# Pooled attention and top-2 adapters on one core: attention closer behind the scores, the up-projection one slot later, small routing groups at both ends, later keys by bf16 transposes, first blocks interleaved

## The chip, the core and the metric

One core of a Trainium2 chip runs the whole program. The metric is device time in microseconds (us) of one execution; each kernel was executed several times, and one execution was recorded by the hardware profiler. The span of the profile (first to last instruction) is 1.7 to 2.4 us shorter than the time of the same execution. On one core a run is called slow when it is over 1.5% above the fastest of the same kernel. PE is the matmul engine (TensorE), DVE VectorE, ACT ScalarE, POOL GpSimd, and SP the queue that issues most DMAs.

## The reference

```python
kv_pool = kv.reshape(B, H//4, 4, W//4, 4, C).mean(axis=(2, 4))   # B=4, 384x32 positions, C=128
k = v = kv_pool.reshape(B, -1, C) @ w_sr                          # 768 keys per batch
a = softmax(q @ k.T / sqrt(C));  x = a @ v                        # 12288 queries per batch
logits = x @ w_gate                                               # 8 experts, the top 2 kept
out = x + sum over the two kept experts of w_e * (x @ A[e]) @ B[e]   # rank 16
```

The kernel handles 512 queries at a time: 96 chunks, numbered 0 to 95, 24 of them per batch.

## The kernel before

The main loop is a sequence of slots. In slot k the scores of chunk k are made, while earlier chunks pass through the later stages. An engine takes its instructions in the order in which they are written down. Cut:

```python
def attend(k, s):        # 6 matmuls for one quarter of the chunk, into the only accumulator buffer
def normalize(k):        # VectorE: reciprocal, multiply -> xn
def top(k):              # VectorE: 4 MAX8, the sorted logits
def route(k0, step):     # a group of (mostly) 4 chunks
    if step == 0:        # GpSimd: two subtractions, one add; ScalarE: tanh; GpSimd: a comparison
    else:                # GpSimd: two multiply/add steps -> gw, the gates
def transposes(kx, kh, tail):  # PE: xn of chunk kx and the gated hg of chunk kh; copied by
                               # VectorE, or by ScalarE in the tail (after the last scores)
def down(k), gate(k)     # PE: x @ A for all experts; VectorE: times the gates -> hg
def up(k), finish(k)     # PE: hg @ B; VectorE: plus xn; store
# ... cut ...
for k in range(LA, last + 2):                 # LA = 4
    ka, kn = k - LA, k - LA - 1               # attention 4 slots behind the scores
    scores(k, 0); normalize(kn); transposes(x_, h_, not ks)
    scores(k, 1); attend(ka, 0); top(kn); route(first[kn], 0)   # route: if a group ends here
    scores(k, 2); up(h_); finish(h_); route(first[kn], 1)
    down(x_); gate(x_); attend(ka, 1..3)
    # ... pooling adds of the next batch on GpSimd, 2 or 3 a slot, in slots 9 to 20 of a batch
    # ... pieces of key preparation at the end of slots 18 to 23 of a batch, one or two a slot
```

(The guards for the first and last slots are left out of this outline.)

The softmax here doesn't subtract the row's maximum and nothing guards it: scores larger than these inputs give would overflow.

## Time and profile before

| | before |
|---|---|
| time, median of the first three runs | 434.14 us |
| span of the profile | 431.2 us |
| PE busy | 401.7 us, 93% |
| VectorE, ScalarE, GpSimd busy | 73%, 68%, 38% |

Two parts of the page of the kernel before: the slices (each digit is the busy share of one of 40 equal slices of the span, in tenths; PEclk is the granted matmul clock in tenths), and the chain of waits that ended last.

```profile
PE   4778999999999999999999999999999999999763
...
PEclk9899999999999999999999999999999999999996
...
PE 78%; DVE 8%; ACT 6%; issue 2%; POOL 2%; SPq 2%; DMA 1%; POOLq 0%; ACTq 0%; DVEq 0%
```

PE is full from about the fourth slice to the 37th. What can be gained lies in the length of a slot, in the first four slices and in the last three.

One plain slot of PE in the timeline of the kernel before. The columns are start, busy time, instructions; the difference of two starts is what a step costs, because matmuls overlap and their ends are modelled.

```profile
59.67 0.59 PE L67 MATMUL sg<-qT,kfT 128*128 128x512 bf16 x2
60.10 0.39 PE L67 MATMUL tt_ps<-id_bf,xn 128*128 128x128 bf16 x4
60.33 0.39 PE L67 MATMUL tt_ps<-id_bf,hg 128*128 128x128 bf16 x4
60.55 0.59 PE L67 MATMUL sg<-qT,kfT 128*128 128x512 bf16 x2
60.98 0.54 PE L67 MATMUL acc<-vx,em 128*128 128x137 f16 x6
61.44 0.59 PE L67 MATMUL sg<-qT,kfT 128*128 128x512 bf16 x2
61.87 0.39 PE L67 MATMUL d_ps<-b_bf,tts 128*128 128x128 bf16 x4
62.09 0.39 PE L67 MATMUL h_ps<-a_bf,tts 128*128 128x128 bf16 x4
62.31 1.28 PE L67 MATMUL acc<-vx,em 128*128 128x137 f16 x18
```

The next slot begins at 63.43, so the slot is 3.76 us. The first six attention matmuls (60.98 to 61.44) take 0.46 us, while eighteen of them take 1.12, that is 0.37 for six: 0.09 are lost, and in the list of waits the weight loads (PEld) wait for the normalised tile (xn) 66 times, for 22.2 us in all.

VectorE's list of waits in the kernel before (total us, times, longest us):

```profile
DVE osb L340 <- PE d_ps L67: 56.0, 94, 1.9
...
DVE hg L327 <- POOL gw L292: 2.2, 3, 1.2
```

VectorE waits for the up-projection (d_ps) in nearly every chunk, and hardly ever for gates (gw).

### The profile page before, as it was taken

To read this page: it belongs to the slowest core of one execution; us is meant where nothing else is said; L and a number is where in the kernel's file an instruction comes from. 1 tells how busy PE (TensorE), PEld (TensorE's weight loads), DVE (VectorE), ACT (ScalarE), POOL (GpSimd) and SP (SyncE) were. 2 spreads that over 40 slices of the span, in tenths; PEclk is the share of its full clock that TensorE was granted. 3 is DMA by queue.
4 is the path that set the end of the run, shared out by engine and by line. 5 is a ranking of instruction groups with operands and counts; after the bars stand their busy time and mean duration, and the time that the engine had idled before them with its cause. 6 is when DMAs were issued, how large, how long until landed. Compare 5 with 4: busy or idle time off the path is not lost.

```text
span 431.2 us, 11431 instructions
## 1 busy us (share of the span) xinstructions
PE 401.7 (93%) x4589; PEld 311.3 (72%) x4589; DVE 315.4 (73%) x916; ACT 293.8 (68%) x335; POOL 165.0 (38%) x263
## 2 busy tenths in 40 slices
PE   4778999999999999999999999999999999999763
PEld 4446677777777787777777787777777778777652
DVE  2442478878777887877878888877878788888863
ACT  3349977857687777757687777767678777777422
POOL 0020278764112369764112369764202202212131
PEclk9899999999999999999999999999999999999996
DMA  8998978997459999997559998977548724422332
GB/s 267 378 244 181 248 183 154 267 176 148 124 122 213 215 270 220 242 213 148 133 114 228 242 299 227 216 162 148 143 104 172 173 74 123 111 63 75 99 98 75
DMA packets 127429, 76.44 MB, mean 177 GB/s; under 512 B 50480, under 2 KB 126512, under 8 KB 127024
## 3 DMA queue, kind: packets, MB, share of 16 engines
q1 hardware_dynamic: 126384, 64.11, 57.6%
q0 software_dynamic: 704, 11.54, 15.7%
q8 instruction: 36, 0.59, 0.6%
q14 instruction: 17, 0.14, 0.1%
q10 hardware_dynamic: 288, 0.07, 0.1%
HBM read 50.53 MB, written 36.70 MB: 202 GB/s over the span
## 4 chain that ended last, share of the span: by engine, by line
PE 78%; DVE 8%; ACT 6%; issue 2%; POOL 2%; SPq 2%; DMA 1%; POOLq 0%; ACTq 0%; DVEq 0%
PE acc L67 31%; PE sg L67 26%; PE tt_ps L67 8%; PE h_ps L67 5%; PE d_ps L67 5%; ACT em L233 4%; DVE xn L250 3%; PE kfT_ps L67 2%; PE kpT_ps L67 1%; SPq L93 1%; DMA kvr<-in_kv_dram 1%; PE v_ps L67 1%; DVE vx L213 1%; ACT tts L311 1%; DVE kpT L197 1%
## 5 line engine op out<-in xcount | busy, mean ns | idle before, releaser
L233 ACT ACTIVATE em<-sg 128x1024 f16<-128x1024 f32 x288 | 274.6, 1023 | 86.3 <-PE sg L67 86.3
L67 PE MATMUL acc<-vx,em 128*128 128x137 f16 x2304 | 174.5, 224 | 3.4 <-DVE xn L250 2.1
L67 PE MATMUL sg<-qT,kfT 128*128 128x512 bf16 x576 | 171.1, 380 | 4.7 <-ACT em L233 2.6
L67 PEld LDWEIGHTS <-em 128*128 128x128 f16 x2304 | 151.7, 98 | 30.8 <-DVE xn L250 19.7
L340 DVE TENSOR_TENSOR osb<-d_ps,xn 128x512 f32<-128x512 f32 x96 | 66.4, 691 | 56.0 <-PE d_ps L67 56.0
L167 POOL TENSOR_TENSOR kvr<-kvr 128x512 f32<-128x512 f32 x63 | 78.2, 1273 | 0.0
L250 DVE TENSOR_TENSOR xn<-acc,rinv 128x544 f32<-128x544 f32 x96 | 69.6, 725 | 3.3
L67 PEld LDWEIGHTS <-tts 128*128 128x128 bf16 x768 | 50.7, 98 | 24.6 <-ACT tts L311 2.1
L327 DVE TENSOR_TENSOR hg<-h_ps,gw 128x512 bf16<-128x512 f32 x96 | 65.4, 681 | 4.0 <-POOL gw L292 2.2
L67 PEld LDWEIGHTS <-kfT 128*128 128x128 bf16 x576 | 49.7, 97 | 17.6 <-issue 6.3
L313 DVE COPY tts<-tt_ps 128x1024 bf16<-128x1024 bf16 (+1 forms) x89 | 60.6, 683 | 0.0
L67 PEld LDWEIGHTS <-xn 128*128 128x128 bf16 x384 | 29.2, 98 | 25.3 <-DVE xn L250 2.5
L67 PE MATMUL tt_ps<-id_bf,xn 128*128 128x128 bf16 x384 | 37.1, 219 | 3.8 <-DVE xn L250 2.2
L67 PE MATMUL d_ps<-b_bf,tts 128*128 128x128 bf16 x384 | 37.4, 220 | 2.0 <-ACT tts L311 1.7
L67 PE MATMUL tt_ps<-id_bf,hg 128*128 128x128 bf16 x384 | 37.2, 220 | 1.5 <-DVE hg L327 1.5
L67 PE MATMUL h_ps<-a_bf,tts 128*128 128x128 bf16 x384 | 37.1, 219 | 0.6 <-ACT tts L311 0.4
L269 DVE MAX8 srt<-xn 128x8 f32<-128x8 f32 x384 | 34.9, 153 | 0.3
L245 DVE RECIPROCAL rinv<-acc 128x4 f32<-128x4 f32 x96 | 17.3, 180 | 17.8 <-PE acc L67 14.3
L67 PEld LDWEIGHTS <-hg 128*128 128x128 bf16 x384 | 25.4, 98 | 2.1 <-DVE hg L327 2.1
L311 ACT COPY tts<-tt_ps 128x1024 bf16<-128x1024 bf16 (+1 forms) x10 | 8.0, 844 | 15.4 <-PE tt_ps L67 12.8
L171 DVE TENSOR_TENSOR kvr<-kvr 128x512 f32<-128x512 f32 x12 | 7.7, 687 | 6.3 <-DMA kvr<-in_kv_dram 6.2
L213 DVE CAST vx<-v_ps 128x272 f16<-128x272 f32 x12 | 5.3, 445 | 9.1 <-PE v_ps L67 9.0
(244 smaller groups left out, 175.0 us busy)
## 6 DMA issues: line engine op xcount, KB each, us to landing
kvr<-in_kv_dram SPq DMA_DIRECT2D x96, 256.0 KB, 5.0
out_dram<-osb SPq DMA_DIRECT2D x96, 256.0 KB, 3.2
qf<-in_q_dram SPq DMA_DIRECT2D x4, 256.0 KB, 5.5
qbf_327<-in_q_dram POOLq DMA_DIRECT2D x1, 512.0 KB, 6.7
qbf_329<-in_q_dram POOLq DMA_DIRECT2D x1, 512.0 KB, 7.8
qbf_548<-in_q_dram POOLq DMA_DIRECT2D x1, 512.0 KB, 10.0
qbf_826<-in_q_dram POOLq DMA_DIRECT2D x1, 512.0 KB, 9.3
qbf_1144<-in_q_dram POOLq DMA_DIRECT2D x1, 512.0 KB, 8.7
```

Source lines behind the costliest of these rows:

```text
L67: return keep(nc.tensor.matmul(*a, **k))
L167: keep(adder.tensor_tensor(u[:, lo:hi], u[:, lo:hi], v[:, lo:hi], op=ALU.add))
L171: keep(adder.tensor_tensor(u, u, v, op=ALU.add))
L213: keep(nc.vector.tensor_copy(vx[b][:, 2 * h:2 * h + 2, 0:VC], ps))
L233: keep(nc.scalar.activation(em[k][:, 2 * r:2 * r + 2], ps, AF.Exp, bias=0.0, scale=scale))
L245: keep(nc.vector.reciprocal(ri, acc[k][:, :, VC]))
L250: keep(nc.vector.tensor_tensor(x, acc[k][:, :, 0:VC], ri.unsqueeze(2).broadcast_to([P, S, VC]), op=ALU.mult))
L269: keep(nc.vector.max(srt[k0][:, m, s], xn[k][:, s, C:VC]))
L311: keep(nc.scalar.copy(sb[:, lo:hi], ps[:, lo:hi]))
L313: keep(nc.vector.tensor_copy(sb[:, lo:hi], ps[:, lo:hi]))
L327: keep(nc.vector.tensor_tensor(hg[k].rearrange("p s (e r) -> p (s e) r", e=E), hp[k].rearrange("p s (e r) -> p (s e) r", e=E), gw[k0][:, m ...
L340: keep(nc.vector.tensor_tensor(osb, dp[k], xn[k][:, :, 0:C], op=ALU.add))
```

## The change

The intent: let every engine find its input ready; start the adapters' work earlier, so that less is left for the tail; and make the keys of later batches more cheaply. The core of the diff, cut:

```diff
-    sizes = [GC] * (NCHUNK // GC - 2) + [2, 2, 2, 1, 1]
+    sizes = [1, 1, 2] + [GC] * (NCHUNK // GC - 6) + [2] * 8 + [1] * 4
 ...
+        def turn(h):                       # keys of later batches: transposes of the bf16 values
+            ps = mtile([P, 2, P], BF16, name="kfT_ps")
+            for i in range(2):
+                mm(ps[:, i], st["vb", h][:, i], id_bf, is_transpose=True, ...)
-            for f in (keys, keys2, values):
+            for f in (keys, keys2, values) if adder is nc.vector else (keys, values, turn):
 ...
-    def route(k0, step):
+    def route(k0):
+        eng = nc.gpsimd if size[k0] > 1 else nc.vector
         # two subtractions, an add and the comparison at once; then:
+        if size[k0] > 1 and k0 > 3:
+            later.append(rest)             # tanh and the last two steps: in the next slot
+        else:
+            rest()
 ...
+    att = {LA: [0], LA + 1: [1], LA + 2: [2, 3], LA + 3: [4, 5], LA + 4: [6, 7]}
+    for k in range(8, NCHUNK):
+        att[k + 1] = [k]                   # from chunk 8 on, one slot behind the scores
 ...
         if ks:
             scores(k, 0)
+        while later:
+            later.pop(0)()
+        for n in kn:
+            normalize(n)
+            if not ks:
+                after_norm(n)              # top and route
-        for x_, h_ in pairs:
+        for x_, h_ in pairs[:1]:
             transposes(x_, h_, not ks)
 ...
             scores(k, 1)
+        for u_ in ku:                      # ku: the chunks whose hg was transposed a slot ago
+            up(u_)
+            finish(u_)
 ...
+        if rest and i in (14, 15, 16, 18, 19, 20, 21, 22, 23):
+            rest.pop(0)()                  # one piece of key preparation per slot
 ...
-        if b + 1 < B and 9 <= i < 21:
-            h, j = divmod(i - 9, 4)
+        if b + 1 < B and 8 <= i < 20:      # the pooling adds, two a slot
+            h, j = divmod(i - 8, 4)
```

Before the main loop, the first scores of each key block are also interleaved with the making of the next block.

More of the change, by code (lines that the diff above doesn't have):

```diff
@@ L54 @@
     ppool = ctx.enter_context(tc.tile_pool(name="ppool", bufs=7))
-    xpool = ctx.enter_context(tc.tile_pool(name="xpool", bufs=4))
-    rpool = ctx.enter_context(tc.tile_pool(name="rpool", bufs=3))
+    xpool = ctx.enter_context(tc.tile_pool(name="xpool", bufs=5))
+    rpool = ctx.enter_context(tc.tile_pool(name="rpool", bufs=4))
+    gpool = ctx.enter_context(tc.tile_pool(name="gpool", bufs=6))
     run = ctx.enter_context(tc.tile_pool(name="run", bufs=3))
@@ L213, in values @@
             keep(nc.vector.tensor_copy(vx[b][:, 2 * h:2 * h + 2, 0:VC], ps))
+            if adder is not nc.vector:
+                st["vb", h] = prep.tile([P, 2, C], BF16, tag="vb", name="vb")
+                keep(nc.vector.tensor_copy(st["vb", h], ps[:, :, 0:C]))
+        def turn(h):
+            ps = mtile([P, 2, P], BF16, name="kfT_ps")
+            for i in range(2):
+                mm(ps[:, i], st["vb", h][:, i], id_bf, is_transpose=True,
+                   start=(i == 0), stop=(i == 1))
+            keep(nc.vector.tensor_copy(kfT[b][:, 2 * h:2 * h + 2], ps))
         for h in range(3):
-            for f in (keys, keys2, values):
+            for f in (keys, keys2, values) if adder is nc.vector else (keys, values, turn):
                 rest.append(lambda h=h, f=f: f(h))
@@ L252, in normalize @@
         xn[k] = x
-    rt = {}
-    sizes = [GC] * (NCHUNK // GC - 2) + [2, 2, 2, 1, 1]
+    sizes = [1, 1, 2] + [GC] * (NCHUNK // GC - 6) + [2] * 8 + [1] * 4
     first, size = {}, {}
@@ L269, in top @@
             keep(nc.vector.max(srt[k0][:, m, s], xn[k][:, s, C:VC]))
-    def route(k0, step):
+    later = []
+    def route(k0):
         n = size[k0] * S
+        eng = nc.gpsimd if size[k0] > 1 else nc.vector
         lg = xg[k0].rearrange("p m s c -> p (m s) c")[:, 0:n, C:VC]
         so = srt[k0].rearrange("p m s e -> p (m s) e")[:, 0:n]
-        if step == 0:
-            def over(i):
-                d = rpool.tile([P, GC * S, 8], FP32, tag=f"over{i}", name=f"over{i}")[:, 0:n]
-                keep(nc.gpsimd.tensor_tensor(
-                    d, lg, so[:, :, i].unsqueeze(2).broadcast_to([P, n, 8]), op=ALU.subtract))
-                return d
-            arg, mask = over(0), over(1)
-            keep(nc.gpsimd.tensor_tensor(arg, arg, mask, op=ALU.add))
-            th = rpool.tile([P, GC * S, 8], FP32, tag="th", name="th")[:, 0:n]
-            keep(nc.scalar.activation(th, arg, AF.Tanh, bias=0.0, scale=0.5))
-            keep(nc.gpsimd.tensor_scalar(mask, mask, 0.0, None, op0=ALU.is_ge))
-            rt[k0] = th, mask
-        else:
-            th, mask = rt.pop(k0)
-            w = rpool.tile([P, GC * S, 8], FP32, tag="gw", name="gw")
-            keep(nc.gpsimd.tensor_tensor(w[:, 0:n], th, mask, op=ALU.mult))
-            keep(nc.gpsimd.tensor_tensor(w[:, 0:n], w[:, 0:n], mask, op=ALU.add))
-            gw[k0] = w
@@ new lines, in over, with rest @@
+        def over(i):
+            d = rpool.tile([P, GC * S, 8], FP32, tag=f"over{i}", name=f"over{i}")[:, 0:n]
+            keep(eng.tensor_tensor(
+                d, lg, so[:, :, i].unsqueeze(2).broadcast_to([P, n, 8]), op=ALU.subtract))
+            return d
+        arg, mask = over(0), over(1)
+        keep(eng.tensor_tensor(arg, arg, mask, op=ALU.add))
+        keep(eng.tensor_scalar(mask, mask, 0.0, None, op0=ALU.is_ge))
+        def rest():
+            gates(k0, n, eng, arg, mask)
+        if size[k0] > 1 and k0 > 3:
+            later.append(rest)
+        else:
+            rest()
@@ L295, in transposes, with gates @@
+    def gates(k0, n, eng, arg, mask):
+        th = rpool.tile([P, GC * S, 8], FP32, tag="th", name="th")[:, 0:n]
+        keep(nc.scalar.activation(th, arg, AF.Tanh, bias=0.0, scale=0.5))
+        w = gpool.tile([P, GC * S, 8], FP32, tag="gw", name="gw")
+        keep(eng.tensor_tensor(w[:, 0:n], th, mask, op=ALU.mult))
+        keep(eng.tensor_tensor(w[:, 0:n], w[:, 0:n], mask, op=ALU.add))
+        gw[k0] = w
     def transposes(kx, kh, tail):
@@ L351 @@
     for h in range(3):
-        for item in sums[h] + rest[3 * h:3 * h + 2]:
+        for item in sums[h]:
             item()
-        for k in range(LA):
-            scores(k, h)
-            if k == 1:
-                rest[3 * h + 2]()
+        rest[3 * h]()
+        if h > 0:
+            scores(2, h - 1)
+        rest[3 * h + 1]()
+        if h > 0:
+            scores(3, h - 1)
+            rest[3 * h - 1]()
+        scores(0, h)
+        scores(1, h)
+    rest[8]()
+    scores(2, 2)
+    scores(3, 2)
     rest = []
@@ L368 @@
     turn_q(1, 0, nc.scalar)
+    att = {LA: [0], LA + 1: [1], LA + 2: [2, 3], LA + 3: [4, 5], LA + 4: [6, 7]}
+    for k in range(8, NCHUNK):
+        att[k + 1] = [k]
+    normed = {}
+    for t, ks in att.items():
+        for k in ks:
+            normed[k] = t + 1 if k == ks[-1] else t
     enter = {}
+    e = 0
     for k in range(NCHUNK):
-        e = first[k] + size[k] + LA + (k - first[k]) + (size[k] == GC)
+        done = normed[first[k] + size[k] - 1]
+        late = k < NCHUNK - 2
+        two = size[k] < GC and (k % 4 == 0 or k > NCHUNK - 4) and len(enter.get(e, [])) < 2
+        e = max(e if two else e + 1, done + late)
         enter.setdefault(e, []).append(k)
@@ L376 @@
     sums, rest = [], []
-    kh = []
-    for k in range(LA, last + 2):
+    kh, ku = [], []
+    for k in range(LA, last + 3):
         b, i = divmod(k, NB)
         ks = k < NCHUNK
-        ka = k - LA if k - LA < NCHUNK else None
-        kn = k - LA - 1 if 0 <= k - LA - 1 < NCHUNK else None
+        ka = att.get(k, [])
         kx = enter.get(k, [])
@@ L397, with after_norm @@
                 load_kv(b + 1, h, j, 1)
+        def after_norm(kn):
+            top(kn)
+            if kn == first[kn] + size[kn] - 1:
+                route(first[kn])
+        kn = [n for n in att.get(k - 1, []) if normed[n] == k]
         if k == LA:
             for s in range(S):
-                attend(ka, s)
-            ka = None
+                attend(0, s)
+            ka = []
         if ks:
             scores(k, 0)
-        if kn is not None:
-            normalize(kn)
+        while later:
[4 more added lines that the diff above has]
+                after_norm(n)
         pairs = [(kx[j] if j < len(kx) else None, kh[j] if j < len(kh) else None)
                  for j in range(max(len(kx), len(kh)))]
-        for x_, h_ in pairs:
+        for x_, h_ in pairs[:1]:
             transposes(x_, h_, not ks)
@@ L413 @@
             scores(k, 1)
-        if ka is not None:
-            attend(ka, 0)
-        ends = kn is not None and kn == first[kn] + size[kn] - 1
-        if kn is not None:
-            top(kn)
-            if ends:
-                route(first[kn], 0)
+        for u_ in ku:
+            up(u_)
+            finish(u_)
+        for a_ in ka[:-1]:
+            for s in range(S):
+                attend(a_, s)
+            normalize(a_)
+            after_norm(a_)
+        if ka and len(ka) == 1:
+            attend(ka[0], 0)
         if ks:
+            for n in kn:
+                after_norm(n)
             scores(k, 2)
-        for h_ in kh[:1]:
-            up(h_)
-            finish(h_)
-        if ends:
-            route(first[kn], 1)
         for x_ in kx[:1]:
@@ L430 @@
             gate(x_)
-        if ka is not None:
-            for s in range(1, S):
-                attend(ka, s)
-        for h_ in kh[1:]:
-            up(h_)
-            finish(h_)
+        if rest and i in (14, 15, 16, 18, 19, 20, 21, 22, 23):
+            rest.pop(0)()
+        for a_ in ka[-1:]:
+            for s in range(1 if len(ka) == 1 else 0, S):
+                attend(a_, s)
+        for x_, h_ in pairs[1:]:
+            transposes(x_, h_, not ks)
         for x_ in kx[1:]:
@@ L439 @@
             gate(x_)
+        ku = kh
+        if not ks:
+            for u_ in ku:
+                up(u_)
+                finish(u_)
+            ku = []
         kh = kx
-        if b + 1 < B and 9 <= i < 21:
-            h, j = divmod(i - 9, 4)
+        if b + 1 < B and 8 <= i < 20:
+            h, j = divmod(i - 8, 4)
             for _ in range(3 if j == 3 else 2):
@@ L445 @@
                     sums[h].pop(0)()
-        if i >= 18 and rest:
-            rest.pop(0)()
-            if len(rest) > NB - 1 - i:
-                rest.pop(0)()
 _INS = ['q', 'kv', 'w_sr', 'moe_w_gate', 'moe_A', 'moe_B']
```

## The prediction

> **What bounds it now.** The slice view has PE at 9 tenths from 40 to about 400 us; the wait list gives PE only about 23 us of waits. The chain of waits is 78% PE. In the timeline a plain chunk repeats every 3.76 us, in start-to-start PE times: three score pairs 0.43 each, 24 attention matmuls 1.49 if unhindered, four MoE blocks of four matmuls 0.22 each. That is 3.66; the rest is the first attention block, 0.46 instead of 0.37, whose weight load waits for the normalised tile. Every fourth (routing) chunk takes 3.93: its tanh waits for GpSimd ahead of an exp. (0.22 us per four 128-column matmuls agrees with the Trainium skill, "TensorE: Matmul & The Clock Gate", "Wait — 56ns, not 53.3ns?".)
>
> Outside that: 34 us before the main loop, with 3 us ScalarE gaps between key blocks; key preparation of three batches, seven slots taking 32.0 us instead of 26.6 (5.4 us each, 3.6 of it PE work); and a tail of 31 us after the last full slot, holding about 13 us of PE work.
>
> **What changes, in PE time.**
> 1. Steady slots: the up-projection now stands before the first attention block, so the normalised tile (ready 1.15 us into the slot) is in time, at 1.52. VectorE no longer waits 0.57 us per slot for the up-projection (56 us in the wait list). The tanh goes behind an exp, a slot later. 3.76/3.93 -> about 3.66: some 8 us over 66 slots.
> 2. Keys: a float32 matmul of 0.48 becomes two bf16 transposes of 0.11, nine times: 3.3 us; one piece per slot removes most stalls. VectorE gets about 0.25 us more per block, which its new slack covers. Together 8 us.
> 3. Start: interleaving brings the main loop 3 us earlier; the double-attention slots 6 to 8 give some back, with one accumulator buffer (about 0.6 us each).
> 4. Tail: 31 -> about 18 us, but 8 us of its work moves forward, and routing on VectorE and double slots cost 2 to 3. Start and tail together: 4 to 5 us.
> 5. Loss: a group's gates are now finished in the slot that uses them, and GpSimd takes two pooling adds (1.24 us each) between the first routing half and its last two multiplies. The Trainium skill (same page, "Architectural detail") says GpSimd is strictly first in, first out. In batches 0 to 2 the routing slots 9, 13 and 17 fall in the pooling window: gates ready about 4.7 us into a slot instead of 2.8, the gating multiply late, its transpose stalling PE about 1.1 us in the next slot. Nine times: 10 us.
>
> **Sum.** 431 - 8 - 8 - 4.5 + 10 = 421 span, plus about 2.9 from span to measured time, less a little for rounding: 422 us, range 413 to 430. Chances: faster by over 2% 0.68, within 2% 0.29, slower 0.03.
>
> **What would show each step.** (1) Plain slots 3.66 apart; VectorE's wait for the up-projection nearly gone. (2) No PE wait on key copies; preparation adding about 2.5 us per batch. (3) First main-loop attention near 31 us instead of 34.4. (4) From the last score matmul to the end about 20 us instead of 33. (5) VectorE waiting on gates about 2 us, nine times, and PE for the gated tile about 1 us each.
>
> **What would make it wrong.** If the pooling adds don't delay the gates, about 412. If VectorE, at about 3.2 us of 3.66 per slot, becomes the limit in key or double slots, or the single accumulator stalls the early double slots longer, 430 or more.

## The result

| | before | after |
|---|---|---|
| time, median (4 runs each) | 433.87 us | 427.49 us |
| range | 431.53 to 434.31 | 426.91 to 427.82 |
| span of the profile | 431.2 us | 425.8 us |
| mean granted clock | 0.988 | 0.976 |

The ratio is 0.9862, 95% interval 0.9825 to 0.99. A ratio is the mean time of one kernel's fast runs over that of the other's in the same rounds, so it isn't quite the ratio of the medians. The gain is 1.4%, about half of the forecast, though the time lies within the stated range.

The same two parts of the page, of the kernel after:

```profile
PE   4798899999999999999999999999999989999753
...
PEclk9999999999999999999999999999999999999955
...
PE 73%; DVE 11%; POOL 5%; ACT 4%; issue 3%; SPq 3%; DMA 1%; ACTq 0%; DVEq 0%; POOLq 0%
```

GpSimd's share of the chain has risen from 2% to 5%, and the clock is at half for the last two slices instead of a part of the last.

A plain slot of PE in the timeline of the kernel after:

```profile
57.12 0.59 PE L68 MATMUL sg<-qT,kfT 128*128 128x512 bf16 x2
57.55 0.39 PE L68 MATMUL tt_ps<-id_bf,xn 128*128 128x128 bf16 x4
57.77 0.39 PE L68 MATMUL tt_ps<-id_bf,hg 128*128 128x128 bf16 x4
58.00 0.59 PE L68 MATMUL sg<-qT,kfT 128*128 128x512 bf16 x2
58.43 0.39 PE L68 MATMUL d_ps<-b_bf,tts 128*128 128x128 bf16 x4
58.65 0.54 PE L68 MATMUL acc<-vx,em 128*128 128x137 f16 x6
59.02 0.38 PE L68 MATMUL sg<-qT,kfT 128*128 128x512 bf16 x1
59.46 0.39 PE L68 MATMUL h_ps<-a_bf,tts 128*128 128x128 bf16 x4
59.68 1.28 PE L68 MATMUL acc<-vx,em 128*128 128x137 f16 x18
60.80 0.59 PE L68 MATMUL sg<-qT,kfT 128*128 128x512 bf16 x2
```

The slot is 3.68 us (57.12 to 60.80), and the six attention matmuls take 0.37. (The single sg at 59.02 is one whose neighbour's record is missing; its start still counts.)

VectorE's waits in the kernel after:

```profile
DVE hg L348 <- POOL gw L313: 10.7, 13, 1.8
...
DVE osb L361 <- PE d_ps L68: 2.6, 3, 1.4
```

The wait for the up-projection is gone, from 56.0 to 2.6 us, and a new one for gates has come. The first slot in which this happens, in the timeline of the kernel after:

```profile
61.85 2.49 POOL L168 TENSOR_TENSOR kvr<-kvr 128x512 f32<-128x512 f32 x2
...
62.41 0.30 ACT L310 ACTIVATE th<-over_840 128x128 f32<-128x128 f32 x1
...
64.31 0.44 POOL L312 TENSOR_TENSOR gw<-th,over_842 128x128 f32<-128x128 f32 x1
...
64.83 0.45 POOL L313 TENSOR_TENSOR gw<-gw,over_842 128x128 f32<-128x128 f32 x1
...
65.32 0.69 DVE L348 TENSOR_TENSOR hg<-h_ps,gw 128x512 bf16<-128x512 f32 x1 [1.81 <-POOL gw L313]
...
66.07 0.40 PE L68 MATMUL tt_ps<-id_bf,hg 128*128 128x128 bf16 x4 [0.77 <-DVE hg L348]
```

Read it downwards: the tanh ended at 62.71, but GpSimd was in two pooling adds until about 64.3; so the gates were ready at 65.3, VectorE stood 1.81 us, and PE waited for the gated tile.

And a stretch of the tail of the kernel after:

```profile
402.39 0.39 PE L68 MATMUL tt_ps<-id_bf,xn 128*128 128x128 bf16 x4
...
402.61 0.39 PE L68 MATMUL tt_ps<-id_bf,hg 128*128 128x128 bf16 x4
...
405.19 0.23 ACT L310 ACTIVATE th<-over_7771 128x32 f32<-128x32 f32 x1 [3.56 <-DVE over_7771 L296]
405.32 0.99 ACT L332 COPY tts<-tt_ps 128x1024 bf16<-128x1024 bf16 x1
...
406.37 0.61 PE L68 MATMUL h_ps<-a_bf,tts 128*128 128x128 bf16 x4 [1.66 <-ACT tts L332]
...
406.77 2.28 PE L68 MATMUL acc<-vx,em 128*128 128x137 f16 x18
```

The transposes are done at 403.0, but ScalarE copies them at 405.32, because a tanh stands before the copy and waits for VectorE's routing. PE then waits for the copy, with the last attention behind. And those 18 attention matmuls take 2.28 us instead of 1.28: the clock has been at half since 405.0.

### Where the time went

A slot's length can be read from the starts of successive normalisations. The main loop's slots 9 to 94 (86 of them) take 344.65 us before and 340.11 after; 86 slots of 3.68 would take 316.5. Measured against that, and with the two ends added:

| part | lost before | lost after | gain | predicted gain |
|---|---|---|---|---|
| plain and routing slots outside key preparation | 7.5 | 0 | 7.5 | 8 |
| key preparation, three batches | 19.0 | 7.8 | 11.2 | 8 |
| pooling adds between the halves of routing | 0 | 10.1 | -10.1 | -10 |
| slots that take two chunks, the two after each, and slot 94 | 1.6 | 5.8 | -4.1 | } |
| start: when slot 9 begins | 52.25 | 57.12 | -4.9 | } together 4.5 |
| from the start of slot 95 to the end | 34.3 | 28.6 | 5.7 | } |

The key and pooling rows of "after" are parted with the first experiment, in which 7.8 of their 17.9 us remain. The 19.0 are all that the 24 slots around key preparation lost before, so some 3 us of plain-slot loss are in that row. The sum of the gains is 5.3 us; the spans differ by 5.4. The start is later because more work is done in it. It is the last three rows together that miss the forecast: 3.3 us lost, where 4.5 were to be gained.

### The profile page after: what moved, and what is told of

It reads as the page before. It is cut to its first block, busy times and chain, and to the rows that moved or that the text cites. A ratio compares the mean times of both kernels' runs of the same rounds, so it can differ in the third digit from the quotient of the medians.

```text
span 425.8 us, 11380 instructions
## 1 busy us (share of the span) xinstructions
PE 386.8 (91%) x4515; PEld 310.2 (73%) x4589; DVE 327.4 (77%) x967; ACT 293.1 (69%) x336; POOL 162.5 (38%) x263
## 4 chain that ended last, share of the span: by engine, by line
PE 73%; DVE 11%; POOL 5%; ACT 4%; issue 3%; SPq 3%; DMA 1%; ACTq 0%; DVEq 0%; POOLq 0%
PE acc L68 30%; PE sg L68 20%; PE tt_ps L68 9%; PE h_ps L68 5%; PE d_ps L68 5%; DVE hg L348 3%; SPq L94 2%; ACT em L244 2%; POOL kvr L168 2%; DVE xn L261 2%; DVE tts L334 1%; DVE osb L361 1%; PE v_ps L68 1%; DMA kvr<-in_kv_dram 1%; DVE rinv L256 1%
## 5 line engine op out<-in xcount | busy, mean ns | idle before, releaser
L244 ACT ACTIVATE em<-sg 128x1024 f16<-128x1024 f32 x288 | 280.7, 1023 | 98.6 <-PE sg L68 68.5
L68 PE MATMUL sg<-qT,kfT 128*128 128x512 bf16 x502 | 154.9, 378 | 2.7 <-ACT em L244 2.2
L68 PEld LDWEIGHTS <-tts 128*128 128x128 bf16 x768 | 59.3, 99 | 53.1 <-ACT tts L332 5.6
L348 DVE TENSOR_TENSOR hg<-h_ps,gw 128x512 bf16<-128x512 f32 x96 | 66.2, 689 | 30.5 <-POOL gw L313 10.7
L334 DVE COPY tts<-tt_ps 128x1024 bf16<-128x1024 bf16 (+1 forms) x95 | 63.9, 673 | 2.4 <-PE tt_ps L68 2.4
L68 PEld LDWEIGHTS <-kfT 128*128 128x128 bf16 x576 | 45.9, 97 | 6.0 <-issue 3.7
L68 PE MATMUL tt_ps<-id_bf,hg 128*128 128x128 bf16 x384 | 38.1, 223 | 3.2 <-DVE hg L348 2.8
L68 PE MATMUL kpT_ps<-id_f,kvr 128*128 128x128 f32 x66 | 11.6, 299 | 1.3 <-DVE kvr L172 1.0
L68 PEld LDWEIGHTS kpT_ps<-id_f,kvr 128*128 128x128 f32 x66 | 7.7, 151 | 3.9 <-DVE kvr L172 3.3
```

The source lines that it names most:

```text
L68: return keep(nc.tensor.matmul(*a, **k))
L244: keep(nc.scalar.activation(em[k][:, 2 * r:2 * r + 2], ps, AF.Exp, bias=0.0, scale=scale))
L334: keep(nc.vector.tensor_copy(sb[:, lo:hi], ps[:, lo:hi]))
L348: keep(nc.vector.tensor_tensor(hg[k].rearrange("p s (e r) -> p (s e) r", e=E), hp[k].rearrange("p s (e r) -> p (s e) r", e=E), gw[k0][:, m ...
```

## The experiments

Theory: the forecast's terms for the slots, the keys and the pooling adds are right, and the tail was mis-sized, because ScalarE's order and the halved clock were overlooked. Rivals: the late gates come from the moved tanh; the tail is bound by VectorE alone; moving attention forward is itself a loss; the interleaved start is absorbed by ScalarE; the cheaper keys are paid for on VectorE.

| run | what it is | time, median of all runs | fast-run ratio to before (95%) | span |
|---|---|---|---|---|
| e1_pool | after, adds out of the way | 420.95 | 0.9643 (0.96 to 0.9686) | 415.2 |
| e2_tailorder | after, tail's ScalarE order | 428.19 | 0.985 (0.9807 to 0.9892) | 428.1 |
| e3_warm | after, unused matmuls in the tail | 429.61 | 0.9906 (0.9875 to 0.9938) | 425.9 |
| e4_lag4 | after, attention four behind | 431.52 | 0.9943 (0.9895 to 0.9992) | 431.3 |
| e5_keys32 | after, float32 keys | 433.12 | 1.0009 (0.996 to 1.0058) | 433.6 |
| e6_oldstart | after, first blocks as before | 432.14 | 0.9967 (0.9932 to 1.0003) | 434.4 |
| e7_uponly | before, up-projection later | 441.79 | 1.0205 (1.0176 to 1.0235) | 440.9 |
| e9_best | after, three repairs | 416.63 | 0.9586 (0.9545 to 0.9626) | 411.7 |
| e10_better | the same, tail mended | 418.93 | 0.9587 (0.9537 to 0.9637) | 418.7 |
| e11_betterwarm | e10 with 8 unused matmuls | 410.96 | 0.9481 (0.9443 to 0.9518) | 419.0 |
| e12_uptanh | before, up-projection and tanh later | 425.59 | 0.9804 (0.9763 to 0.9846) | 424.0 |
| e13_early_q | e11, queries loaded earlier | 410.32 | 0.9502 (0.9469 to 0.9535) | 408.6 |

All gave correct results. Some of the profiled executions were several us longer than the median of their kernel, by delays that are no effect of the edits (see e13_early_q). So stretches of the profiles are compared below (the starts of the normalisations, and the tail, counted from the start of the last exp to the end: 32.0 us before, 25.2 after), not whole spans.

### e1_pool: no pooling add in a routing slot

```diff
-            for _ in range(3 if j == 3 else 2):
+            for _ in range((3, 0, 3, 2)[j]):
```

> The changed kernel, but with no pooling add issued in the slots in which a routing group ends (3, 0, 3 and 2 adds in each four slots instead of 2, 2, 2 and 2). Theory (GpSimd's in-order adds between the two halves of the routing cost 1.15 us of PE time nine times): profiled span 425.8 -> about 415.5, VectorE's wait for gates 10.7 -> under 2 us, PE's wait for the gated tile 7.8 -> under 1.5 us. Rival (the gates are late because their tanh was put behind an exp a slot later, and the adds only fill time in which GpSimd waits): waits for gates stay over 5 us, span at 423 or more.

Measured: from the ninth to the 80th normalisation 269.05 us instead of 279.16, 10.1 us less, 1.12 for each of nine slots. PE's wait for the gated tile fell from 7.8 us to 0.5. VectorE's wait for gates in this run's list:

```profile
DVE hg L348 <- POOL gw L313: 6.8, 18, 0.4
```

It is 6.8 us, more than the 2 us expected: each gate is still up to 0.4 us late. But that fits into VectorE's slack and PE doesn't wait for it. The moved tanh alone is thus not the cause: it takes the pooling adds between the halves of the routing. Of the four runs two were slow (423.8 and 425.8 us), the others 417.0 and 418.1.

### e2_tailorder: routing after the transposes in the tail

```diff
             normalize(n)
-            if not ks:
-                after_norm(n)
         for x_, h_ in pairs[:1]:
             transposes(x_, h_, not ks)
+        if not ks:
+            for n in kn:
+                after_norm(n)
```

> The changed kernel, but after the last scores a chunk's routing is issued after the transposes of its slot instead of before them. Theory (in the tail the ScalarE copy of the transposes stood 2.2 us in the queue behind a tanh that waited for VectorE's routing, and the late copy idled PE): span 425.8 -> 422 to 424, the ScalarE copy of slot 96 starts at about 403.2 instead of 405.3, the clock may fall later too. Rival (the tail is bound by VectorE's own queue, in which the last normalisation stands behind gates and finishes): within 0.7 us of 425.8.

The tail took 22.05 us instead of 25.2. In the timeline of this run:

```profile
408.03 0.39 PE L68 MATMUL tt_ps<-id_bf,hg 128*128 128x128 bf16 x4
...
408.45 1.01 ACT L332 COPY tts<-tt_ps 128x1024 bf16<-128x1024 bf16 x1 [1.41 <-PE tt_ps L68]
...
410.60 0.23 ACT L310 ACTIVATE th<-over 128x32 f32<-128x32 f32 x1 [1.14 <-DVE over L296]
```

The copy follows the transposes at once and the tanh comes after it. The clock fell later too, 11.3 us after the last exp began instead of 4.4. So ScalarE's order cost 3.1 us of tail against the profile of the kernel after, the part of the halved clock that it brought about included. Three other profiles with the tail's code unchanged (e1_pool, e5_keys32, e6_oldstart) have tails of 24.3 to 24.5 us, so the cost is rather 2.3 to 3.1. The whole span doesn't show it: in this run the clock was at half for 6.8 us at the start, which put the loop 2.3 us later, and two slots of the last pooling window were longer by 3.0 us. The timed ratio is that of the changed kernel, and the verdict rests on the tail of the profile alone.

### e3_warm: unused matmuls where PE waits in the tail

```diff
+    def warm_pe(k, n):
+        if k < NCHUNK - 1:
+            return
+        ps = ps_s.tile([P, 2, T], FP32, tag="sg", name="idle")
+        for i in range(n):
+            mm(ps[:, i % 2], kfT[B - 1][:, 0], qT[NCHUNK // GC - 1][:, 0:T], start=True, stop=True)
     # three or four of them before up, before the first down and before the second down
```

> The changed kernel, with about 40 unused 512-column matmuls put where PE waits after the last scores, so that PE stays busy. Nothing reads them. Theory (the clock fell to half at 405 us, because PE was mostly idle for 3.4 us before, and the halved matmuls are on the tail's chain): granted clock 1.0 to within some 4 us of the end, the 18 attention matmuls of the last chunk 1.1 us instead of 2.2, span 2 to 3 us shorter. Rival (the tail is a chain through VectorE and ScalarE in which PE's rate matters little): less than 0.8 us, or a loss because the extra matmuls get in the way.

The stretches before and after the clock's fall in the kernel after (columns: from:to, length, busy us and instructions of PE, weight loads, VectorE, ScalarE and GpSimd, then the clock, the DMA share and GB/s), and the like of this run:

```profile
398.20:401.60 3.40, 2.79 (x39) 2.34 (x37) 3.12 (x14) 2.23 (x4) 0.00 (x0) 1.00 0.26 77
401.60:405.00 3.40, 1.76 (x22) 1.34 (x22) 2.77 (x12) 0.03 (x1) 0.00 (x0) 1.00 0.00 0
405.00:408.40 3.40, 2.03 (x19) 2.03 (x20) 1.95 (x6) 1.13 (x2) 0.00 (x0) 0.51 0.27 77
```

```profile
401.80:405.20 3.40, 2.79 (x30) 1.83 (x29) 2.77 (x12) 0.02 (x1) 0.00 (x0) 1.00 0.00 0
405.20:408.60 3.40, 2.56 (x34) 2.00 (x34) 1.95 (x6) 1.17 (x3) 0.00 (x0) 1.00 0.26 77
408.60:412.00 3.40, 1.80 (x15) 0.89 (x14) 1.93 (x4) 0.98 (x1) 0.00 (x0) 1.00 0.03 8
```

With PE kept busy the clock stayed full until 412.2, the 18 attention matmuls took 1.28 us, and the last chunk was normalised 11.05 us after the last exp began instead of 13.01. So the halved clock did cost 2.0 us by that point. (In e1_pool, e5_keys32 and e6_oldstart, with the same tail code as the kernel after, the figure is 12.3 to 12.4: the clock fell there 5.1 to 6.4 us after the last exp, and in two of them it was full again for a while. Against those the gain is 1.3.) But the tail ended no sooner (25.1): further on the extra matmuls themselves stood in the way, one group of seven holding up the last down-projection by over a microsecond. Over the whole run the edit is no gain; the cost of the clock is shown, the cure isn't.

### e4_lag4: attention four slots behind again

```diff
-    att = {LA: [0], LA + 1: [1], LA + 2: [2, 3], LA + 3: [4, 5], LA + 4: [6, 7]}
-    for k in range(8, NCHUNK):
-        att[k + 1] = [k]
+    att = {k + LA: [k] for k in range(NCHUNK)}
-    sizes = [1, 1, 2] + [GC] * (NCHUNK // GC - 6) + [2] * 8 + [1] * 4
+    sizes = [GC] * (NCHUNK // GC - 2) + [2, 2, 2, 1, 1]
```

> The changed kernel with attention four slots behind the scores and the routing groups of before; keys, up-projection, gates and first blocks as changed. Theory (bringing attention forward moved about 7 us of work from the tail to the double-attention slots at the start, where it cost 4.9 us, and brought stalls in the two-chunk slots near the end, so it gained little): span 422 to 428. If the move is the source of the gain: 430 or more. If it is a net loss: below 422.

The routing groups of before go back with it, so the run tests both together. The last exp began 10.7 us earlier than in the changed kernel (389.95 against 400.62), and the tail was 16.2 us longer (41.4 against 25.2). So it is a trade, and it favours the change, by 5.5 us in the profiles. That span (431.3) is outside what the theory expected, and by the letter of the expectation it says that the move is the source of the gain. However, the clock was at half for 6.8 us at the start there, two slots of the last pooling window were 3.7 us longer there than the same slots a batch earlier, while PE waited 1.9 us for queries, and the two other fast runs had spans of 426.7 and 427.9. How much the move gains isn't settled: some 1 to 5 us. That it is a net loss is refuted.

### e5_keys32: the float32 keys at the new places

```diff
-            if adder is not nc.vector:
-                st["vb", h] = prep.tile([P, 2, C], BF16, tag="vb", name="vb")
-                keep(nc.vector.tensor_copy(st["vb", h], ps[:, :, 0:C]))
-            for f in (keys, keys2, values) if adder is nc.vector else (keys, values, turn):
+            for f in (keys, keys2, values) if adder is nc.vector else (keys, values, keys2):
```

> The changed kernel, but the later batches' keys made by the float32 matmul of before (0.48 us of PE) at the places where the changed kernel transposes bf16 values (0.11 us), and no bf16 copy of the values. Theory (the cheaper keys are worth their PE time, and the extra VectorE copy of 0.42 us is free): each of the nine key slots 0.37 us longer, so rows 8 to 72 of the chunk sequence about 3.3 us longer than in the changed kernel. Rival (VectorE is as tight as PE there, and its extra copy gives the gain back): less than 1 us.

From the ninth to the 57th normalisation, with six of the nine key blocks, 190.81 us instead of 188.55: 2.26 more, 0.38 a block, as the theory has it. For nine that is 3.4. (The stretch ends there because later two slots of this run were longer by 4.8 us for another reason.) Of the 11.2 us gained in the key slots the cheaper keys are thus 3.4. How the rest divides can be read from e12_uptanh (below), which has the old keys at the old places: its 24 slots around key preparation lose 13.4 us, where the kernel before loses 19.0. So 5.6 came with the moves of the up-projection and the tanh alone, and about 2.2 are left for the spacing of the pieces.

### e6_oldstart: the first blocks as before

```diff
-        for item in sums[h]:
+        for item in sums[h] + rest[3 * h:3 * h + 2]:
             item()
-        rest[3 * h]()
-        if h > 0:
-            scores(2, h - 1)
-        # ... and so on: the rest of block h among scores of blocks h - 1 and h
+        for k in range(LA):
+            scores(k, h)
+            if k == 1:
+                rest[3 * h + 2]()
```

> The changed kernel with the first key blocks and first scores in the order of before. Theory (interleaving brings the main loop 3 us earlier, and all of it lasts): the ninth normalisation comes 2.5 to 3.2 us later than in the changed kernel (61.0 us there, if the clock at the start is the same). Rival (the first main-loop slots are bound by ScalarE, so an earlier start is mostly waited away): less than 1.2 us later.

The edit puts the old loop over key blocks back: all of a block's pieces, then four score groups. The ninth normalisation came at 63.37 us instead of 61.00, and the clock at the start was full in both. So 2.4 of the 3 us last into the main loop. The profiled run was a slow one, but the start of it, which is what counts here, was undisturbed.

### e7_uponly: the up-projection's move alone

```diff
             scores(k, 1)
+        for u_ in ku:
+            up(u_)
+            finish(u_)
         if ka is not None:
             attend(ka, 0)
...
-        for h_ in kh[:1]:
-            up(h_)
-            finish(h_)
```

> The kernel before, with only the up-projection moved a slot later, in front of the first attention block. Theory (the normalised tile is then in time and VectorE stops waiting for the up-projection): plain slots 3.68 instead of 3.76 us, VectorE's wait for it 56 -> under 8 us, and the stalls around key preparation shrink a little with VectorE's new slack; routing slots still longer by about 0.17. Over the run 5 to 9 us shorter. Rival (the plain slot is bound elsewhere, for instance by the exps): 3.74 or more.

Plain slots went to 3.68 as expected, but routing slots to 4.57 instead of 3.94, and the kernel is 2% slower than before (1.8 to 2.3%). Of this run, ScalarE's list of waits:

```profile
ACT th L285 <- POOL over L283: 39.7, 26, 2.2
```

and one line of PE's timeline in a routing slot:

```profile
68.91 0.59 PE L67 MATMUL sg<-qT,kfT 128*128 128x512 bf16 x2 [0.73 <-ACT em L233]
```

VectorE now does the finish first and comes to the MAX8 later; GpSimd starts later; the tanh, which stands before the next exps, holds ScalarE up 1.54 us; and the exp that would free the scores' PSUM is late. The tail is longer as well, 35.9 instead of 32.0. VectorE's wait for the up-projection fell only to 19.1 us, not under 8.

### e12_uptanh: the up-projection and the tanh moved together

To e7_uponly is added: the tanh and the last two GpSimd steps of a group of four are issued in the next slot, behind its first exp, and the pooling adds as 2, 2, 4 and 0.

```diff
-            th = rpool.tile([P, GC * S, 8], FP32, tag="th", name="th")[:, 0:n]
-            keep(nc.scalar.activation(th, arg, AF.Tanh, bias=0.0, scale=0.5))
-            rt[k0] = th, mask
+            rt[k0] = arg, mask              # the tanh moves into the second step
...
             scores(k, 0)
+        for k0 in list(rt):
+            route(k0, 1)
```

> The kernel before with the up-projection a slot later, and with the tanh and last two multiplies of a routing group of four moved to the next slot, behind its first exp; pooling adds issued 2, 2, 4 and 0 so that none comes between. Theory (the up-projection's move alone lost because VectorE then reaches the routing later and the tanh holds up the exps; the two moves belong together): routing slots 3.68 to 3.75 instead of 4.57, so plain and routing slots alike, and the main loop (fifth to 85th normalisation) about 20 us shorter than with the up-projection's move alone, and some 8 to 10 us shorter than in the kernel before; the tail longer than before by several us, because the up-projection comes a slot later there too. Rival (the routing slots stay long for another reason): 4.2 or more.

Routing slots became 3.68 like the plain ones. From the fifth to the 85th normalisation: 307.5 us, against 323.1 with the up-projection's move alone and 320.2 before. The gain of 12.7 on the kernel before is more than the 8 to 10 expected, the 15.6 on e7_uponly less than 20. The tail is longer, 36.1 us. So the up-projection's move pays only together with the other two edits; the tanh's move alone was not run. This accounts for the steady part of the change without the earlier attention, new keys or new groups.

### e9_best, e10_better: repairs put together

e9_best has the edit of e1_pool, that of e2_tailorder, and two more: in slots that take two chunks the second transposes stand before the last three attention blocks, and the last chunk is normalised straight after its attention.

```diff
+        for x_, h_ in pairs[1:]:
+            transposes(x_, h_, not ks)
         for a_ in ka[-1:]:
             for s in range(1 if len(ka) == 1 else 0, S):
                 attend(a_, s)
-        for x_, h_ in pairs[1:]:
-            transposes(x_, h_, not ks)
+            if not ks:
+                normalize(a_)
```

> The changed kernel with three repairs: pooling adds kept out of the slots where a routing group ends; after the last scores, routing after the transposes and the last chunk's normalisation straight after its attention; and in slots that take two chunks, the second transposes before the last three attention blocks, so that PE does not wait for their copy. If the repairs add up: 10 us from the first, 4 to 6 from the tail, about 0.6 in each of three double slots: span about 409 to 411, time 411 to 414. If the tail is bound by something else, 415 or more.

The span was 411.7, the fast runs 412.3 to 417.2 us, so only two of the four were within the 411 to 414 expected. The slots that take two chunks fell from 5.50 to 4.81 us, and the slot after each from 3.90 to 3.72: 0.87 for each of two. The tail was 22.0, no better than in e2_tailorder: the transposes that were now ahead of the last attention waited 1.58 us for a PSUM buffer. So e10_better keeps them behind it once the scores are over:

```diff
-        for x_, h_ in pairs[1:]:
-            transposes(x_, h_, not ks)
+        if ks:
+            for x_, h_ in pairs[1:]:
+                transposes(x_, h_, False)
         # ... and after the attention:
+        if not ks:
+            for x_, h_ in pairs[1:]:
+                transposes(x_, h_, True)
```

> As the repaired kernel of the run before, but after the last scores the second transposes of a slot stay behind the last attention, since in that run they waited 1.6 us for their PSUM buffer with the attention behind them. Theory (the tail is set by how soon the last chunk is normalised): normalisation of the last chunk 5.5 to 7 us after its last exp began instead of 9.0, tail from that exp to the end 19 to 20.5 us instead of 22.0, span 409 to 410 if the start is the same. Rival (the tail is bound by the chain of copies and gates of the chunks before): tail within 0.7 us of 22.0.

The last chunk was normalised 6.36 us after the last exp began, and the tail was 20.2 us. Three of its six runs were slow, the profiled one among them (its delay lies before the tail). The mended tail doesn't show in the times: the ratio is that of e9_best, and the fast runs are 413.8 to 417.4 us. It rests on this one profile, and on that of e13_early_q, whose tail is 20.2 too.

### e11_betterwarm: eight unused matmuls

```diff
+        if k == NCHUNK:
+            warm_pe(k, 2)                  # warm_pe as in e3_warm
         for u_ in ku:
             up(u_)
...
+        if kx[1:]:
+            warm_pe(k, 3)
         for x_ in kx[1:]:
             down(x_)
```

That is three before the second down of slots 95 and 96, and two before the ups of slot 96.

> As the kernel beside it, with 8 unused 512-column matmuls in three places in slots 95 and 96 where PE waits in any case. Theory (the halved clock of the tail costs real time, and it is brought on by PE's waits there): the clock stays at 1.0 at least 3 us longer, the tail 0.8 to 2 us shorter. Rival (PE's rate does not matter in the tail): within 0.4 us.

The tail was 19.8 us, 0.4 less than 20.2, and the clock fell 11.6 us after the last exp began instead of 10.1. That is the rival's range; and e13_early_q, with the same tail and the same unused matmuls, took 20.2 us. So with the order mended no gain of the unused matmuls is shown. (The profiles of e10_better and e11_betterwarm are of slow runs, whose delay lies before the tail.) Yet the fast runs, 410.3 to 412.1 us, are all below the fast runs of e10_better, 413.8 to 417.4. The tail doesn't explain that; milder cases of the delay of the next section may, but those runs weren't profiled, so it stays open.

### e13_early_q: queries loaded earlier

In the slow profile of e11_betterwarm, PE's list of waits and the landing times of the transposing query loads (min, median, max) have these lines:

```profile
PE sg L68 <- DMA qT<-qbf: 5.1, 2, 3.7
```

```profile
DMA to landing us min/median/max: 4.0/6.9/18.5
```

A load is issued at most four slots, some 15 us, ahead of its first use. The edit issues both the cast and the load of every group four slots earlier:

```diff
-            if 2 <= g + 1 < B * NG:
-                load_qT(g + 1)
-            if 4 <= g + 2 < B * NG and g + 2 not in q_bf:
-                cast_q(g + 2)
+            for n in (2, 3) if g == 1 else (g + 2,):
+                if n < B * NG:
+                    load_qT(n)
+            if g + 3 < B * NG:
+                cast_q(g + 3)
```

> As the repaired kernel with the 8 unused matmuls, with the cast and the transposing load of every group of queries issued four slots earlier. Theory (the runs 7 to 10 us longer, two of seven for that kernel, come from a transposing load that lands up to 18.5 us after its issue where some 15 us of lead were given, so that PE waits for queries): no run over 414 us, the profile without a PE wait for a query load, median 410 to 412. Rival (the late data are the key-value loads or something else): slow runs in a third or more, as before.

All six runs lie between 410.0 and 413.3 us, none slow, and PE's list of waits has no transposing load left. With two slow runs in seven before, six clean ones are no proof by count alone; and the profiled run here is a fast one, and the fast profiles of e1_pool, e3_warm and e9_best have no such wait either. So late queries are supported as a cause of this kernel's slow runs (5.1 us of the some 8 by which its slots in the pooling windows are longer), but not shown to be the only one. The kept traces speak against one cause for all: in the slow profile of e10_better no wait is for a transposing load, and PE stood for 5.19 us amid the attention matmuls of one chunk without a wait that the profile names; in e2_tailorder GpSimd waited 6.9 us for key and value loads before the longest slot. The slow runs of e1_pool and e9_best weren't profiled. This version is the fastest of all, 0.9502 of the kernel before; the changed kernel is 0.9862 of it.

## Why the prediction was right or wrong

The time was within the range, and the verdict that was thought likelier, faster by over 2%, did not come. That the time still lay in the range is in part luck: the loop gave 2.7 us more than forecast, which made up for a part of the 7.8 us that the tail, the start and the two-chunk slots fell short. Without these 2.7 it would have been 430.2, just outside.

1. **Steady slots: right.** Forecast 3.66 and some 8 us; measured 3.68 and 7.5. VectorE's wait for the up-projection went from 56.0 to 2.6 us. e12_uptanh shows it with these moves alone. What the prediction listed as a small extra, the later tanh, is a condition: without it (e7_uponly) the up-projection's move loses 2%.
2. **Keys: right, and undersized.** Forecast 8 us, measured 11.2; the cheaper keys alone are 3.4 (e5_keys32), as forecast (3.3). But half of the 11.2, 5.6 us, belongs to the moves of point 1 (e12_uptanh), and only about 2.2 to the spacing. What preparation still adds, 7.8 us or 2.6 a batch, is as forecast (2.5).
3. **Start: as forecast as far as it was singled out.** The first main-loop attention came at 31.02 us (forecast: near 31), and 2.4 us of the interleaving last (e6_oldstart). But slot 9 begins 4.9 us later than before, because more work is done by then.
4. **Tail: the step that failed.** The prediction said "31 -> about 18 us" and "from the last score matmul to the end about 20 us"; measured 25.2 (from the last exp, a count that gives 32.0 for the kernel before) and 27.0. It is the mis-sized term: together with the start and the slots that take two chunks it was to give 4 to 5 us, and the three took 3.3. The two-chunk slots and slot 94 cost 4.1 of that. What it had overlooked: the copies of the transposes stand behind the tanh on ScalarE, which waits for VectorE (2.3 to 3.1 us, e2_tailorder); and the waits of PE halve its clock (1.3 to 2.0 us until the last normalisation, e3_warm, in part the same microseconds). With that order and the places of the last normalisation and transposes mended in e10_better the tail is 20.2 us; the 2 us from there to the forecast 18 stay open. The Trainium skill gives a reason to look at the clock: "TensorE: Matmul & The Clock Gate", section "What's actually happening", gives 3.4 us as the window after which an idle PE runs at half; the records here do change in windows of 3.413 us, though PE wasn't idle in the window before the fall but busy for about half of it (1.76 us).
5. **Pooling adds: right in mechanism and size.** Forecast nine times 1.1 us, 10 in all; measured 10.1 (e1_pool). This rested on one statement of the Trainium skill ("TensorE: Matmul & The Clock Gate", section "Architectural detail"), that GpSimd is strictly first in, first out, which the timeline of the kernel after agrees with (the gates' multiply began only at 64.31, when two adds were done), and on two durations of the trace before.

So the halved gain is no hidden contention in the loop: what the loop gained, 18.7 us, it gave back in the pooling slots (10.1, as forecast) and at the two ends and in the two-chunk slots (3.3, where 4.5 were to be gained).

## What to carry to other kernels

A step that is moved to a later slot keeps its place in its engine's queue only relative to what is written there: for each moved step, list what the same engine does just before it now, and whether that can wait for another engine. Here such a look foretold the pooling adds to the microsecond, and leaving it out for the tail, where a copy stood behind a waiting tanh, left that term wrong. And read the length of a slot from the starts of a step that occurs once in each: it tells effects of 0.1 us apart, where run times differ by several us for other reasons.

## What the Trainium skill lacked or had wrong

- "TensorE: Matmul & The Clock Gate" (sections "What's actually happening", "HAM oscillation — how this bites in real kernels" and "A second HAM failure mode: psum-queue depth-cycling") has the clock fall after an idle window and speaks of gaps over 3.4 us, and of short waits that are frequent enough, without a figure for these. In the tail of the changed kernel it fell after a window of 3.4 us in which PE was busy for 1.76 us and no wait ended that was longer than 1.2 us. No page says how busy a window has to be. The profile's busy time doesn't tell it: in windows cut at the steps of the clock record, the clock fell after 1.76 us and was kept after 1.54 (e11_betterwarm, from 178.7 us). What does tell the windows of all 14 traces apart, from 20 us on and without those with float32 matmuls, is how many columns the matmuls stream in a window, transposes included: the 22 windows at full clock after which it fell had at most 2,870 columns, and the 1,202 after which it was kept at least 2,870; of the windows at half clock, the 7 after which it rose had at least 3,362, and the 39 after which it stayed at most 2,567. Without the transposes they are not apart: it fell after 2,560 columns (e3_warm, from 408.8 us) and was kept after 1,617 (the kernel before, from 414.2). (A plain slot of 3.68 us streams 8,408. Some records are missing, so the limit is rough.)
- "DMA: Bandwidth & Descriptors" gives bandwidths for transposing loads, but no spread of their latency under load: 4.0 to 18.5 us, median 6.9, in e11_betterwarm, which decides how early one has to be issued.
- "TensorE: Matmul & The Clock Gate" (section "What's actually happening") does say that the slow start varies from run to run with the phase of the window. It has no figure for what varied here: none, one or two windows at half clock after one or two full ones. In the profiles with the start of the kernel after, the ninth normalisation came at 60.6 to 61.1 us with none (after, e3_warm, e10_better, e13_early_q), at 61.3 to 61.8 with 3.4 us at half (e1_pool, e5_keys32, e9_best) and at 63.1 to 63.3 with 6.8 (e2_tailorder, e11_betterwarm).
